# A top-k attention and its MLP on one core: the last two pairs of a batch alternate by chunk, row blocks are joined across pairs

## The chip, the cores and the metric

The kernel runs on one core of a Trainium2 chip. The metric is the device time of one execution in microseconds. Before the change it is 878.69 us as the median of three runs (876.53 to 879.49).

The engines have short names in this document: PE (TensorE, matmul), DVE (VectorE), ACT (ScalarE), POOL (GpSimd) and SP (SyncE, here only a queue that issues DMAs). "PEld" is PE's loading of weights.

## What is computed

Eight batches of eight heads, 576 rows, 64 columns a head. Each row of scores keeps its 32 largest entries; the softmax over these weighs v. The heads of a row are put side by side to 512 columns, and an MLP with 2048 hidden columns and one slope per hidden column (a leaky ReLU) follows.

```python
scores = scale * np.matmul(q, k.transpose(0, 1, 3, 2))
kth = np.partition(scores, -top_k, axis=-1)[..., -top_k:-top_k + 1]
mask = scores >= kth
scores = np.where(mask, scores, -1000000000.0)
scores = scores - np.max(scores, axis=-1, keepdims=True)
attn = np.exp(scores)
attn = attn / (np.sum(attn, axis=-1, keepdims=True) + 1e-09)
return np.matmul(attn, v).astype(np.float32)
...
h = x @ w_in
g = np.maximum(h, 0.0) + alpha * np.minimum(h, 0.0)
return (g @ w_out).astype(np.float32)
```

## The kernel before

**Tiles.** Heads are handled in pairs: 32 pairs, four to a batch. A pair has nine tiles of 128 score rows by 576 columns: tiles 0 to 7 are the four 128-row chunks of its two heads in turn (`j // 2` is the chunk, `j % 2` the head), and tile 8, which the text also calls row block 8, holds the last 64 rows of both heads. There are 288 tiles, and `ORDER[n]` says which pair and which row block tile `n` is. For batches zero to six the order is pair after pair; in the last batch the four pairs are mixed by chunk.

**One tile's way.** PE computes its scores into PSUM (`scores`, L326). ACT writes `b` = scores plus a row's estimated threshold (`act_b`, L335; `NT0` is the estimate), then takes the sign of `b` with a sum over the row, which counts how many entries are above the estimate (`act_s`, the tile `h`, L341), and later the exponential `e` (`act_e`, L346). POOL makes a sign flag `SG` of the count (`side_of`, L351). DVE makes `y` from `b` and `SG` (`flip`, L357), takes the eight largest of six segments of `y` (`seg_ops`, L367), merges them (`merge_ops`, L382 and L384), picks the row's exact limit (L395 to L411) and writes the mask `mk` (L431). POOL multiplies mask and exponential to the weights `w` (L441; DVE does it for the last six tiles, L438). SP issues a DMA that transposes two tiles of `w` (L454; L449 and L450 for row block 8). PE multiplies the transposed weights with v, and with a column of ones that gives the row's sum (`av`, tile `pu`, L489); DVE takes the reciprocal of the sums (`av_rz`, L506 and L508), and ACT scales the product into `xb` (`av_out`, L518). `x_turn` has SP issue the transposes of `xb` into `xT`, the MLP's input.

**Turns.** The order of all instructions is written out by hand: a loop over turns `n` (L765) emits, for each engine, the steps due in that turn. Turn `n` has the scores of a following tile, `b` and `h` of tile `n`, `y` of tile `n - 1`, the segments of tile `n - 2`, the merge of tile `n - 3`, and mask and weights of tile `n - 7`. Each engine works through its own list in that order and waits only where an operand or a buffer is not ready, so ACT and PE may run ahead of DVE. That distance is called ACT's lead.

**Units.** `act_b` and `act_e` run on units of one or two tiles. Before, a unit never crosses from one pair to the next, so nine tiles make four units of two and one of one (in the last batch some of row block 8 are joined). Scores of a unit are issued in the turn before it. Units of two share five buffers of `b` and four of `e`; units of one have a buffer of each of their own.

**Preparation of a pair.** `prep_plan` transposes q and k (`pe_q`, `pe_k`, `pe_t`, copied by `act_q`, `act_k`, `act_t` into one of `NQ = 5` buffers `qkT`), estimates the thresholds (`pe_g` to `dve_6`), and converts v (`act_v`). The list `ts` has the turn of each step relative to the pair's base turn `BASE[p]`. Slot "dvx" stands behind `flip` in a turn of DVE, slot "dve" ahead of it. Loads of q and k are issued 18 turns and loads of v (`load_v`) 13 turns ahead of the base turn, v into two stages in turn.

**The MLP.** Its steps wait in a queue `back`, one block of rows after another: `ph` steps (the hidden columns, L644, with ACT's `gT`, L650) and `pz` steps (the output, L658 and L662, with ACT's `o_sb`, L667). `feed(lim)` puts every block whose rows are complete into the queue. The loop takes one step a turn, and from turn 254 on up to two, within a credit of 1.9 us a turn. Batch six has two blocks of 256 rows and leaves 64 rows, which form a block with 64 rows of the last batch. `tail_of` plans the products, reciprocals, outputs and transposes of a tile after its weights, and calls `feed`. For batch six before: chunks 0 and 1 are complete with tile 3 of pair 27, the rest with its tile 8.

**PSUM.** `ps_s` has two tiles of two banks for scores; `ps_m` and `ps_a` have one bank each, for the MLP and for the preparation; `ps_d` has two banks for `pu`, `pr0`, `pr1` and `st`.

## Time and profile before

| | |
|---|---|
| runs | 876.53, 879.49, 878.69 us; median 878.69 us |
| the profiled execution | 875.27 us, its span 873.2 us |
| mean granted PE clock | 0.919 |
| matmuls, weight loads | 5747, 5747 |
| HBM read, written | 36.71 MB, 9.44 MB |

The span runs from the first to the last instruction of the profiled execution. "Busy" is time in which an engine executes; a row of a view of groups gives the source line, the engine, the operation, what is written and read, the count, then the busy time, the mean of one in ns, and behind the second bar the idle time just before these instructions and what ended it. In a view in order of time a row gives start, duration, engine, line and operation; the bracket at its end holds the idle time before it and what ended that. In a view of waits the columns are the sum, the number and the longest.

### The profile page before, as it was taken

The numbers are of one execution on the slowest core, as the hardware profiler recorded it, in microseconds if no ns is written. First come the engines' busy times: TensorE is split into PE (matmuls) and PEld (weight loads), VectorE is DVE, ScalarE is ACT, GpSimd is POOL, SyncE is SP. The second block draws the span as 40 slices with busy tenths as digits, with TensorE's granted clock in tenths as the row PEclk, the third lists the DMA queues.
The fourth block names the chain that finished last, engine by engine and source line by source line (L and its number), as shares of the span: only waits on it lengthen the run. The fifth ranks groups of instructions, "written<-read, shape, count | busy, mean of one in ns | idle before, by whom it ended". The sixth has DMA issues, their size and how long they took to land.

```text
span 873.2 us, 20627 instructions
## 1 busy us (share of the span) xinstructions
PE 725.9 (83%) x5747; PEld 426.9 (49%) x5747; DVE 833.7 (95%) x5185; ACT 789.7 (90%) x1873; POOL 430.1 (49%) x629
## 2 busy tenths in 40 slices
PE   6677687878968799878997789977897989899995
PEld 4344454434544355544454345634455555556663
DVE  4999999999999999999999999999999999999990
ACT  6999999899999999899998999999999999879851
POOL 1455455555545555545555554555554555555520
PEclk9666789699989999899987999999999999899998
DMA  7899644644666445555576456465456564355451
GB/s 163 154 180 204 122 96 92 128 95 88 147 129 116 90 109 120 114 117 95 118 159 116 83 104 132 104 129 101 101 118 123 112 101 100 80 96 101 81 99 41
DMA packets 343019, 99.50 MB, mean 114 GB/s; under 512 B 335200, under 2 KB 335216, under 8 KB 342896
## 3 DMA queue, kind: packets, MB, share of 16 engines
q1 hardware_dynamic: 340544, 95.71, 55.0%
q0 software_dynamic: 1152, 2.10, 1.9%
q8 instruction: 47, 0.77, 0.4%
q14 instruction: 76, 0.62, 0.3%
q10 hardware_dynamic: 1200, 0.30, 0.2%
HBM read 36.71 MB, written 9.44 MB: 53 GB/s over the span
## 4 chain that ended last, share of the span: by engine, by line
DVE 70%; ACT 13%; PE 12%; DMA 2%; issue 1%; POOL 1%; SPq 0%; DVEq 0%
DVE C L367 23%; DVE y L357 11%; DVE mk L431 10%; DVE C L384 9%; DVE L L382 8%; PE pz L662 3%; PE ps L326 3%; ACT b L335 3%; ACT h L341 3%; ACT e L346 2%; PE ph L644 2%; DVE P L244 2%; ACT gT L650 1%; DVE L L401 1%; DVE KK L405 1%
## 5 line engine op out<-in xcount | busy, mean ns | idle before, releaser
L441 POOL TENSOR_TENSOR w<-mk,e 128x576 bf16<-128x576 bf16 x250 | 318.9, 1276 | 336.5 <-DVE mk L431 183.9
L367 DVE MAX8 C<-y 128x8 f32<-128x96 f32 x1728 | 420.8, 244 | 0.1
L326 PE MATMUL ps<-qkT 64*128 64x288 f32 (+1 forms) x1280 | 253.8, 471 | 36.1 <-ACT b L335 35.9
L341 ACT ACTIVATE h<-b 128x576 bf16<-128x576 f32 x288 | 202.8, 704 | 1.6
L335 ACT ACTIVATE b<-ps,NT 128x576 f32<-128x576 f32 x288 | 202.0, 759 | 2.2 <-PE ps L326 2.1
L644 PE MATMUL ph<-xT,w_in_b 128*128 128x128 bf16 (+2 forms) x1088 | 158.5, 294 | 42.2 <-ACT gT L650 35.2
L326 PEld LDWEIGHTS ps<-qkT 64*128 64x128 f32 (+1 forms) x1280 | 133.6, 192 | 96.4 <-ACT b L335 60.1
L346 ACT ACTIVATE e<-b 128x1152 bf16<-128x1152 f32 (+1 forms) x158 | 174.1, 1102 | 0.0
L382 DVE MAX8 L<-C 128x8 f32<-128x48 f32 x864 | 163.5, 189 | 0.1
L357 DVE TENSOR_SCALAR y<-b,SG 128x576 int32<-128x576 int32 x288 | 147.1, 511 | 7.2 <-POOL SG L351 6.8
L431 DVE TENSOR_SCALAR mk<-b,KP 128x576 bf16<-128x576 f32 x282 | 143.8, 510 | 0.0
L644 PEld LDWEIGHTS <-w_in_b 128*128 128x128 bf16 x1088 | 85.7, 101 | 108.5 <-issue 80.0
L662 PE MATMUL pz<-w_out_b,gT 128*128 128x512 bf16 x576 | 138.6, 380 | 0.0
L650 ACT ACTIVATE gT<-ph 128x512 bf16<-128x512 f32 x144 | 88.0, 618 | 37.8 <-PE ph L644 37.6
L384 DVE MATCH_REPLACE8 C<-L,C 128x48 f32<-128x48 f32 x576 | 108.9, 189 | 0.0
L662 PEld LDWEIGHTS <-gT 128*128 128x128 bf16 x576 | 53.2, 98 | 70.6 <-issue 14.0
L489 PE MATMUL pu<-v_bf,wT 128*128 128x65 bf16 (+1 forms) x1600 | 69.6, 198 | 10.4 <-DMA wT<-w 6.8
L489 PEld LDWEIGHTS <-wT 128*128 128x128 bf16 (+1 forms) x1600 | 65.0, 103 | 21.4 <-DMA wT<-w 8.1
L351 POOL TENSOR_SCALAR SG<-S_all 128x1 int32<-128x1 f32 x288 | 64.6, 224 | 17.6 <-ACT h L341 17.5
L441 POOL TENSOR_TENSOR wm<-mk,e 128x576 bf16<-128x576 bf16 x32 | 40.8, 1275 | 49.9 <-DVE mk L431 47.1
L341 ACT ACTIVATION_READ_ACCUMULATOR h<-b 128x1 f32 x288 | 62.6, 217 | 0.0
L518 ACT ACTIVATE xb<-pu,rz 128x64 bf16<-128x64 f32 x224 | 54.3, 367 | 0.0
(100 smaller groups left out, 711.8 us busy)
## 6 DMA issues: line engine op xcount, KB each, us to landing
out_dram<-o_sb SPq DMA_DIRECT2D x35, 256.0 KB, 2.4
st_q<-in_q_dram SPq DMA_DIRECT2D x64, 128.0 KB, 2.9
st_v<-in_v_dram SPq DMA_DIRECT2D x64, 128.0 KB, 2.6
kst<-in_k_dram SPq DMA_DIRECT2D x62, 128.0 KB, 2.7
w_stage<-in_moe_w_out_dram SPq DMA_DIRECT2D x16, 256.0 KB, 3.1
w_in_b<-in_moe_w_in_dram POOLq DMA_DIRECT2D x8, 256.0 KB, 6.2
wT<-w SPq DMA_TRANSPOSE x128, 3.3
st_q<-in_q_dram SPq DMA_DIRECT2D x32, 32.0 KB, 2.7
```

Of the source, the lines that this page charges most:

```text
L326: nc.tensor.matmul(o_, l_, r_, start=True, stop=True)
L335: nc.scalar.activation(t["b"].rearrange("p (a c) -> p a c", a=2), t["ps"], AF.Identity, bias=NT0[:, p * TPP + j:p * TPP + j + 1], scale=ON ...
L341: nc.scalar.activation(h, tiles[n]["b"], AF.Sign, accum_out=S_all[:, n:n + 1])
L346: nc.scalar.activation(e, tiles[n0]["bu"], AF.Exp, scale=scl)
L357: nc.vector.tensor_scalar(t["y"].bitcast(I32), t["b"].bitcast(I32), FLIP, SG[:, n:n + 1], ALU.bitwise_xor, ALU.bitwise_xor)
L367: return [lambda g=g: nc.vector.max(out=C[:, n % TPP, g, :], in_=t["y"][:, g * SEG:(g + 1) * SEG]) for g in range(NSEG)]
L382: ops.append(lambda r=r, src=src: nc.vector.max(out=L[:, 8 * r:8 * r + 8], in_=src))
L384: ops.append(lambda r=r, src=src: nc.vector.match_replace(out=C2, in_to_replace=L[:, 8 * r:8 * r + 8], in_values=src, imm_value=NEG))
L431: nc.vector.tensor_scalar(t["mk"], t["b"], row_limit(n), None, ALU.is_ge)
L441: nc.gpsimd.tensor_tensor(dst, t["mk"], t["e"], ALU.mult)
L644: nc.tensor.matmul(hold[f][:, i, :], w_in_b[:, kk, (f + i) * 128:(f + i + 1) * 128], xT[:, kk, c0:c0 + tb], start=(kk == 0), stop=(kk == N ...
L662: nc.tensor.matmul(pz[0:m], hold["gT"][:, f, r0:r0 + m], w_out_b[:, f, :], start=False, stop=(f == NFT - 1))
```

## The change

1. `ORDER`: pairs 26 and 27 (`PA`, `PA + 1`), the last two of batch six, alternate by chunk: tiles 2i and 2i+1 of pair 26, the same of pair 27, for i from 0 to 3; then row block 8 of both.
2. `av_alt`, `rz_alt` and `out_alt` handle one chunk of both pairs at a time (20 matmuls in one `pu` bank), and `tail_of` transposes each chunk at once and feeds the MLP behind chunks 1, 3 and 4.
3. Units are two tiles throughout, except tile 8 of the first pair and the last tile; they cross pairs. `b` has five and `e` four buffers of two tiles, and none of one.
4. `NQ = 6`, one stage for v instead of two, loads of v issued later where the stage demands it, alpha's stage taken from the pool `stage`, `pr0` of the last pair in the pool `ps_a`.
5. `dve_6` in slot "dvx" of turn -3 instead of "dve" of turn -2; `act_v` of pair 1 in its turn -4 instead of 1.

```diff
-    st_vs = [prep.tile([128, 10, D], FP32, name=f"st_v{i}", bufs=1) for i in range(2)]
+    st_v = prep.tile([128, 10, D], FP32, name="st_v", bufs=1)
...
-    NQ = 5
+    NQ = 6
...
-    ORDER = [divmod(n, TPP) for n in range(N0)]
+    ORDER = [divmod(n, TPP) for n in range(N0 - 2 * TPP)]
+    PA = P0 - 2
+    ORDER += [(p, 2 * i + h) for i in range(4) for p in (PA, PA + 1) for h in range(2)]
+    ORDER += [(PA, 8), (PA + 1, 8)]
...
-        m = 1 if ORDER[n][1] == 8 and ORDER[n + 1][1] != 8 else 2
+        m = 1 if n in (8, NT - 1) else 2
...
-            if nm == "pr0":
+            if nm == "pr0" and p < NPAIR - 1:
...
-            ts = [-9, -8, -7, -6, -5, -4, -3, -2, -2, -2, -2, -2, -1, -1, 1]
+            ts = [-9, -8, -7, -6, -5, -4, -3, -2, -2, -2, -2, -2, -1, -1, -4]
...
-            ts = [-14, -13, -12, -11, -10, -9, -7, -6, -5, -5, -4, -4, -3, -2, -8]
+            ts = [-14, -13, -12, -11, -10, -9, -7, -6, -5, -5, -4, -4, -3, -3, -8]
...
-                 dict(dve=[dve_6]), dict(act=[act_v])]
+                 {dvx: [dve_6]}, dict(act=[act_v])]
...
-        b = attn.tile([128, m, S], FP32, name=f"b{m}", bufs=5 if m == 2 else 1)
+        b = attn.tile([128, 2, S], FP32, name="b", bufs=5)
...
-        e = attn.tile([128, m, S], BF16, name=f"e{m}", bufs=4 if m == 2 else 1)
-        nc.scalar.activation(e, tiles[n0]["bu"], AF.Exp, scale=scl)
+        e = attn.tile([128, 2, S], BF16, name="e", bufs=4)
+        nc.scalar.activation(e[:, 0:m, :], tiles[n0]["bu"], AF.Exp, scale=scl)
...
+    def av_alt(i):
+        m = 128 if i < 4 else 64
+        pul[i] = pu = ps_d.tile([128, 4, V1], FP32, name="pu", tag="pd")
+        for s in range(2):
+            d = pairs[PA + s]
+            for side in range(2):
+                cs = slice(0, 128) if i < 4 else slice(64 * side, 64 * side + 64)
+                av_one(pu[0:m, 2 * s + side, :], d, d["wT", i] if i < 4 else d["wTm"], side, cs)
+
+    def rz_alt(i):
+        m = 128 if i < 4 else 64
+        rz = attn.tile([128, 6], FP32, name="rz", bufs=4)
+        nc.vector.reciprocal(rz[0:m, 0:4], pul[i][0:m, :, D])
+        pul[i] = pul[i], rz
+
+    def out_alt(i):
+        m = 128 if i < 4 else 64
+        pu, rz = pul.pop(i)
+        dst = xb[B - 2][i] if i < 4 else xm[B - 2]
+        for c in range(4):
+            nc.scalar.activation(dst[:, 256 + 64 * c:320 + 64 * c], pu[0:m, c, 0:D], AF.Copy,
+                                 scale=rz[0:m, c:c + 1])
...
-            a16 = mlp.tile([NFT, 128], FP32, name="a16", bufs=1)
+            a16 = mlp.tile([128, DM], FP32, name="a16", tag="stage", bufs=3)[0:NFT, 0:128]
...
-            if wp < P0:
+            if wp in (PA, PA + 1):
+                if (wj == 8 or wj % 2) and wp == PA + 1:
+                    i = wj // 2
+                    put(n + 3, "pe", lambda: av_alt(i))
+                    put(n + 4, "dve", lambda: rz_alt(i))
+                    put(n + 6, "act", lambda: out_alt(i))
+                    put(n + 6, "end", lambda: x_turn(b, (i,)))
+                    if i in (1, 3, 4):
+                        lim = (b + 1) * S if i == 4 else b * S + 128 * i + 128
+                        put(n + 8, "end", lambda: feed(lim))
+            elif wp < P0:
...
-        load_v(1)
...
+            if n == 1:
+                load_v(1)
...
-                if n == max(0, BASE[p] - 13):
+                if n == max(BASE[p] - 13, BASE[p - 1] - 7 + 4 * (p == 2)):
```

More of the change, by code (lines that the diff above doesn't have):

```diff
@@ L119, in early_sets @@
             nc.gpsimd.memset(ksts[i][64:128, 4, :], 0.0)
-        for t_ in st_vs:
-            nc.vector.memset(t_[64:128, 4, :], 0.0)
-            nc.vector.memset(t_[0:64, 5, :], 0.0)
+        nc.vector.memset(st_v[64:128, 4, :], 0.0)
+        nc.vector.memset(st_v[0:64, 5, :], 0.0)
         for t_ in v_bfs:
@@ L200, in act_v @@
         def act_v():
-            nc.scalar.copy(d["v"][:, :, 0:D], d["st_v"])
+            nc.scalar.copy(d["v"][:, :, 0:D], st_v)
         def pe_k():
```

5 lines of the change are left out of this document (2 added, 3 removed).

## The prediction

> **What bounds the kernel now.** I read the page's busy shares first, then busy time by stretch, then what VectorE (DVE) waits for, then TensorE (PE) and ScalarE (ACT) in order of time around 760 us.
>
> ```profile
> span 873.2 us, 20627 instructions
> PE 725.9 (83%) x5747; PEld 426.9 (49%) x5747; DVE 833.7 (95%) x5185; ACT 789.7 (90%) x1873; POOL 430.1 (49%) x629
> ...
> 20.00:100.00 80.00, 58.37 (x353) 34.73 (x351) 77.53 (x477) 79.18 (x177) 40.59 (x61) 0.65 0.92 172
> ...
> 300.00:400.00 100.00, 85.53 (x669) 48.04 (x668) 100.00 (x630) 92.94 (x228) 53.07 (x76) 0.95 0.55 111
> ...
> 740.00:770.00 30.00, 25.91 (x243) 17.43 (x239) 29.80 (x189) 25.69 (x59) 15.68 (x24) 0.89 0.40 85
> 770.00:800.00 30.00, 27.18 (x210) 17.05 (x207) 28.69 (x173) 26.57 (x59) 15.90 (x25) 1.00 0.58 104
> 800.00:830.00 30.00, 29.99 (x315) 19.49 (x314) 29.42 (x182) 26.46 (x54) 15.73 (x22) 1.00 0.46 88
> ```
>
> The stretches' columns are PE, PE loads, DVE, ACT and POOL busy, then PE's granted clock. DVE has no gap in the middle of the kernel (100.00 of 100 us). What DVE does not use lies at the start, in the stretches from 740 us on, and behind its last product. So an edit can shorten the kernel only where it removes DVE work, a DVE wait, or a piece of the end. ACT with 92.94 us and PE with 85.53 us in the middle are hidden behind DVE. The waits of DVE, by the instruction that waited; the first row is from 20 to 50 us, the next two from 50 to 100 us (and what PE itself waited for there), then one row for 100 to 740 us and two for 740 to 850 us:
>
> ```profile
> DVE y L357 <- POOL SG L351: 2.4, 1, 2.4
> ...
> DVE rz L506 <- PE pu L489: 1.0, 1, 1.0
> DVE P L244 <- PE pr L236: 0.4, 1, 0.4
> ...
> PE pu L489 <- DMA wT<-w: 3.5, 1, 3.5
> ...
> L357 DVE TENSOR_SCALAR y<-b,SG 128x576 int32<-128x576 int32 x224 | 114.2, 510 | 0.1
> ...
> L357 DVE TENSOR_SCALAR y<-b,SG 128x576 int32<-128x576 int32 x35 | 17.9, 512 | 1.3 <-POOL SG L351 1.1
> ...
> L535 DVE RECIPROCAL rz<-pu 128x4 f32<-128x4 f32 (+1 forms) x9 | 1.5, 171 | 0.8 <-PE pu L489 0.8
> ```
>
> One y per tile: 640 us for 224 tiles is 2.86 us of DVE a tile, which is the length of a turn of the hand-written order. Late DVE waits sum to 1.3 + 0.8 = 2.1 us; after the start-up (y of the first tiles) only 2.4, 1.0 and 0.4 us more are lost. How far ACT is ahead of DVE comes from counting ACT's h and DVE's y begun by 738, 768 and 790 us:
>
> ```profile
> L341 ACT ACTIVATE h<-b 128x576 bf16<-128x576 f32 x254 | 179.1, 705 | 1.5
> L357 DVE TENSOR_SCALAR y<-b,SG 128x576 int32<-128x576 int32 x252 | 128.7, 511 | 5.9 <-POOL SG L351 5.7
> ...
> L341 ACT ACTIVATE h<-b 128x576 bf16<-128x576 f32 x264 | 186.0, 705 | 1.5
> L357 DVE TENSOR_SCALAR y<-b,SG 128x576 int32<-128x576 int32 x263 | 134.3, 511 | 6.1 <-POOL SG L351 5.9
> ...
> L341 ACT ACTIVATE h<-b 128x576 bf16<-128x576 f32 x271 | 190.9, 704 | 1.6
> L357 DVE TENSOR_SCALAR y<-b,SG 128x576 int32<-128x576 int32 x271 | 138.4, 511 | 7.1 <-POOL SG L351 6.8
> ```
>
> The lead is two tiles at 738 us, one at 768 and none at 790: this is the only place after the start where ACT and PE cannot keep up, and it is where the change moves the MLP of batch six (counted from zero). PE there, in order of time, with two stretches:
>
> ```profile
> 747.79 1.62 PE L326 MATMUL ps<-qkT 64*64 64x288 f32 x12
> ...
> 752.13 1.86 PE L326 MATMUL ps<-qkT 64*128 64x288 f32 x8 [1.32 <-ACT b L335]
> 756.77 2.92 PE L326 MATMUL ps<-qkT 64*128 64x288 f32 x8 [2.77 <-ACT b L335]
> 759.62 3.11 PE L644 MATMUL ph<-xT,w_in_b 128*128 128x256 bf16 x16
> ...
> 769.34 0.80 PE L489 MATMUL pu<-v_bf,wT 128*128 128x65 bf16 x20
> 770.07 1.24 PE L326 MATMUL ps<-qkT 64*128 64x288 f32 x8
> 771.24 1.92 PE L644 MATMUL ph<-xT,w_in_b 128*128 128x256 bf16 x16
> ...
> 784.02 2.98 PE L662 MATMUL pz<-w_out_b,gT 128*128 128x512 bf16 x13
> ...
> 750.00:762.00 12.00, 7.91 (x32) 4.67 (x31) 11.80 (x74) 11.12 (x26) 6.44 (x10) 0.72 0.59 119
> 762.00:774.00 12.00, 11.16 (x128) 8.66 (x127) 12.00 (x77) 9.58 (x23) 6.79 (x10) 1.00 0.44 65
> ```
>
> Between two blocks of the MLP, PE has nothing but scores, sits idle (1.32 and 2.77 us), its clock falls to 0.72, and the same eight score matmuls take 2.92 instead of 1.24 us, the same sixteen ph 3.11 instead of 1.92 us. Then two blocks come at once.
>
> **The change part by part.** Durations are from this execution, 875.27 us with its span of 873.2 us. The median of the runs shown, 878.69 us, lies 3.42 us higher; I put the sum on the execution and move the result to the median.
>
> *Batch six fed by chunks.* In the order of the instructions the two 256-row blocks start in turns 258 and 266 instead of 262 and 268, because pairs 26 and 27 finish a chunk every four turns. PE's work per four turns, by the rows above (0.12 us per ph, 0.229 per pz, 0.04 per pu matmul, scores 1.24 a unit, 1.62 with a tile of row block 8), against 4 x 2.86 = 11.4 us of DVE:
> - Before, turns 258 to 261: scores only, 2.5. Then 262 to 265: 64 ph 7.7 + 50 pu 2.0 + scores 3.4 = 13.1; 266 to 269: 40 pz 9.2 + 2.5 + 0.8 = 12.5. PE falls behind by 2.8 us in eight turns, after losing 1.7 + 1.2 + 0.6 = 3.5 us to the clock in the gap.
> - After, 258 to 261: 64 ph 7.7 + 40 pu 1.6 + scores 2.9 = 12.2; 262 to 265: 34 pz 7.8 + 1.6 + 3.2 = 12.6; 266 to 269: 6 pz and 56 ph 8.1 + 0.8 + 2.5 = 11.4; 270 to 273: 34 pz and 8 ph 8.8 + 3.3 = 12.1; 274 to 277, last batch's 128-row block: 10.4. Behind by 2.0 after eight turns, 2.7 at the worst.
>
> So the trough is the same size but is not preceded by a lost 3.5 us, and not by a rest either. Starting from a lead of one tile or a little less, DVE still touches zero. I keep half of the waits: -1.0 us. Ends: -2.1 (all gone), and +0.8: before, a tally of 2.8 us used up a lead of two tiles, at most 5.7 us and by my estimate 4.8, so ACT and PE waiting for one another cost 2 us that the tally does not see; 2.7 + 2 with a lead of 1.8 makes 2.9 us of waits instead of 2.1.
>
> What is queued behind: chunks' x transposes stand on SP four turns before the first ph that reads them (three before), among the transposes of w, and hold them only until ACT has written the chunk, on which ACT is ahead. Same number of transposes.
>
> *Chunk-wise attention products.* Five av of 20 matmuls instead of two pairs of 20 and 30: equal matmuls, equal ACT outputs (20). DVE loses one reciprocal: six (two of the row's form and a small one for each pair) become five:
>
> ```profile
> L506 DVE RECIPROCAL rz<-pu 128x4 f32<-128x4 f32 x56 | 8.0, 144 | 1.0 <-PE pu L489 1.0
> ```
>
> -0.1 us, on the path since DVE is the bound there.
>
> *Row blocks two by two across pairs.* Thirteen pairs of single exponentials become double ones:
>
> ```profile
> L346 ACT ACTIVATE e<-b 128x1152 bf16<-128x1152 f32 x130 | 155.3, 1194 | 0.0
> L346 ACT ACTIVATE e<-b 128x576 bf16<-128x576 f32 x28 | 18.9, 673 | 0.0
> ```
>
> 13 x (2 x 673 - 1194) = 2.0 us of ACT over the whole kernel, hidden by DVE: 0. The lead pays nothing, it grows; bounds 0 and -0.4 (the 0.4 us wait of P between 50 and 100 us, where ACT is busiest, 79.18 of the 80 us from 20 us on). The threshold of a pair's first tile is now needed one turn earlier and is written one turn earlier (dve_6): 0.
>
> *Fewer buffers.* b for ten tiles instead of eleven, e for eight instead of nine. An exponential now waits for POOL's product seven tiles back:
>
> ```profile
> L441 POOL TENSOR_TENSOR w<-mk,e 128x576 bf16<-128x576 bf16 x250 | 318.9, 1276 | 336.5 <-DVE mk L431 183.9
> ```
>
> That product ends, by my count of turns, 1.3 us and a mask after a turn's start, three turns before the y of the unit's second tile: ACT can lead by 3 x 2.86 less about 1.9, so 6.5 us. The lead counted above, two tiles or at most 5.7 us, is under it: 0. If the lead were clipped where a block starts, it would be clipped where it is longest, and DVE would wait only for what a dip takes beyond 6.5 us; no row after 100 us shows even a wait with today's dips.
>
> *One v stage, alpha in the stage pool, load_v later, act_v of pair 1 earlier.* SP issues v of pair 1 after q and k of pair 2; ACT reads it four turns later, so the transposes of w behind it on SP (the first in turn 8) see a queue that is free again. One v copy moves from turn 10 to turn 5 on ACT; its cover is ACT's lead over DVE there. Two memsets less, while DVE waits for the first pair anyway. 0; with the cover gone, one copy:
>
> ```profile
> L201 ACT CAST v_bf<-st_v 128x640 bf16<-128x640 f32 x32 | 23.2, 730 | 1.3 <-DVE NT L286 1.3
> ```
>
> +0.7 us; the other end is -0.4, for the 2.4 us wait at the start if SP's earlier alpha took something off it.
>
> *Six qkT buffers, pr0 of the last pair in another bank*: needed by the new order, no instruction more: 0.
>
> *The end.* The last six tiles, their products and the last block keep their order:
>
> ```profile
> 848.52 4.50 DMA wT<-w
> ...
> 857.24 5.55 PE ph L644 x64
> ```
>
> The end from the last product at 848.5 us is a chain of transposes and one block that waits for no backlog: 0.
>
> Sum: -1.0 - 0.1 = -1.1 us: 874.2 us by the profiled execution, **877.6 us** by the median. Own range, from -2.2 and +0.8: 876.5 to 879.5.
>
> **A rule against the row.** The Trainium skill, "TensorE: Matmul & The Clock Gate", section "The HAM clock gate (the "warmup" mystery)", says that PE drops to half rate after an idle window of about 3.4 us. No single wait in the rows above reaches it (1.32, 2.77 us), yet the clock read 0.72; the measurement decides, and I take the gaps as the cause. By the letter the slow stretch would have another cause and stay, and the 12.2 us of turns 258 to 261 would take 12.2 / 0.72 = 16.9 us, a way into the third rival.
>
> **The rivals.**
> 1. *All waits go* (faster). With PE never idle at 750 us and ACT 2 us lighter, late waits of 2.1 vanish and those between 50 and 100 us (1.0 + 0.4) too: -2.1 - 0.1 - 1.4 = -3.6, 875.1 us. For: the 3.5 us that PE lost to its clock, and ACT's small lead in the first 100 us. Against: the 1.0 us goes back to PE's wait for a transpose of w, not to ACT, and PE's tally stays behind DVE's.
> 2. *The early feed does nothing.* ph would wait for its xT: no chunk gains, 878.6 us. Against: in the late stretch PE waited for xT nowhere but at the last chunks, with three turns of room.
> 3. *ACT and PE set the pace from turn 258* (slower). Between 768 and 790 us ACT did seven tiles in 22 us, 3.14 us a tile. If it keeps that pace for all sixteen turns 258 to 273, DVE loses 16 x (3.14 - 2.86) = 4.5 us, and the gap that restored the lead is gone. Less a lead under 0.3 us, and with 0.8 us of waits left behind it, waits become 5.0 instead of 2.1: +2.9 - 0.1, 881.5 us. It decides when the lead at turn 258 is under a tenth of a tile. For: ACT carries six gT, four outputs and two units in turns 258 to 261. Its units show what that is:
>
> ```profile
> 774.23 1.09 ACT L650 ACTIVATE gT<-ph 128x512 bf16<-128x512 f32 x2
> 775.18 1.39 ACT L335 ACTIVATE b<-ps,NT 128x576 f32<-128x576 f32 x2
> 779.00 0.28 ACT L390 ACTIVATE ra<-S_all,c 128x3 f32<-128x3 f32 x1
> ```
>
> Two gT take 0.95 us and a unit 3.8, so 2.9 + 7.6 + about 1.6 for outputs and the small ones = 12.1 us against 11.4. Against: the pace of 3.14 came while PE ran two blocks at once.
>
> **How the numbers follow.** About 0.3% (2.6 us) is what can be told from no change. Forecast 0.42 and rival 2 0.10 lie inside: same 0.52. Rival 1 0.28: faster. Rival 3 0.20: slower. The range reaches to rivals 1 and 3, widened by the 0.4 us of the small unknowns: 874.6 to 882.0 us.
>
> **What would show it.** Right: PE's clock in the stretch 750 to 762 us near 1.0 and its busy share near 12 of 12; sixteen ph of the first block at 1.9 us; DVE waits after 740 us about 1 us; the middle at 100 of 100. The chunk step is wrong if DVE's y waits for POOL's SG in 755 to 800 us by more than 2 us. The buffer step is wrong if ACT's e shows idle time before POOL and DVE shows any between 100 and 740 us. The whole is wrong if the end behind the last product is not 24 to 25 us, or if DVE's busy sum moves by more than 1 us from 833.7.

## The result and the profile after

The change makes the kernel slower: 885.53 us as the median of nine runs (882.32 to 893.02), beside 878.03 us (876.53 to 882.11) for the kernel before on the same chip. The ratio of the runs is 1.0069, 95% interval 1.0046 to 1.0091, so about 6.1 us (4.0 to 8.0); the two medians are 7.5 us apart. The profiled execution took 885.53 us; its span is 10.6 us longer than the one shown of before, whose execution, at 875.27 us, was faster than all nine runs.

The head of the page of the kernel after:

```profile
span 883.8 us, 20598 instructions
PE 746.4 (84%) x5747; PEld 426.7 (48%) x5747; DVE 835.5 (95%) x5182; ACT 788.3 (89%) x1860; POOL 431.0 (49%) x629
```

With the same 5747 matmuls PE is busy 20.5 us longer, and with three instructions fewer DVE is busy 1.8 us longer; ACT saves 1.4 us. Busy time by stretch (columns as in the prediction) and DVE's waits from 100 to 740 and from 740 to 850 us:

```profile
300.00:400.00 100.00, 89.06 (x687) 48.72 (x687) 100.00 (x624) 91.16 (x221) 52.41 (x75) 0.93 0.56 113
400.00:500.00 100.00, 83.44 (x637) 45.62 (x637) 97.40 (x608) 93.42 (x231) 50.07 (x71) 0.93 0.58 115
740.00:770.00 30.00, 29.32 (x281) 19.22 (x278) 29.88 (x184) 26.86 (x61) 15.65 (x23) 1.00 0.50 98
750.00:762.00 12.00, 12.00 (x85) 5.97 (x82) 11.88 (x79) 9.40 (x26) 6.93 (x11) 1.00 0.55 87
770.00:800.00 30.00, 29.88 (x226) 17.36 (x224) 26.21 (x163) 26.02 (x59) 14.75 (x22) 1.00 0.46 85
...
DVE y L358 <- POOL SG L352: 3.1, 2, 2.6
...
DVE rz L559 <- PE pu L490: 3.7, 1, 3.7
```

The PE clock at 750 us is 1.00 and PE has no gap there, as forecast. But DVE now loses 2.6 us in the middle of the kernel (97.40 of 100), and one 3.7 us wait between 770 and 800 us.

To see where the 10.6 us lie, I cut each trace by the starts of DVE's y of tiles 36, 252 and 287. Before, the cuts are at 119.8, 738.0 and 838.7 us; after, at 122.8, 746.1 and 848.6 us. So 3.0 us come before tile 36, 5.1 in the middle (618.2 us becomes 623.3), 1.8 in the late stage (100.7 becomes 102.5) and 0.75 behind the last y. The first, third and fourth of these are in large part chance, or can't be told from it. Experiments 9 and 10, which do the same work there as the kernel before or a little more, reach tile 36 at 121.4 and 121.1 us. The late stage takes 102.9, 100.9 and 102.0 us in experiments 6, 9 and 10, which have it as before; behind the last y it takes 34.9 and 33.0 us in 6 and 9, beside 34.5 before and 35.2 after.

### Three readings of the trace

**The joined unit is dear.** PE in order of time in the middle of the kernel before (row block 8 alone), then in the kernel of experiment 14, where the same tiles are multiplied alone:

```profile
384.50 1.24 PE L326 MATMUL ps<-qkT 64*128 64x288 f32 x8
390.68 1.19 PE L326 MATMUL ps<-qkT 64*64 64x288 f32 x8
```

```profile
393.16 1.24 PE L328 MATMUL ps<-qkT 64*128 64x288 f32 x4
395.56 1.19 PE L328 MATMUL ps<-qkT 64*64 64x288 f32 x8
```

Eight matmuls of two ordinary tiles, one for each side of the pair and so on different halves of PE's rows, take 1.24 us; the four of a single tile, all on one half, take 1.24 us as well. So two on different halves run at once, and two on one half do not. A unit that joins row block 8 with an ordinary tile would so cost about 1.24 + 1.19 us; at full clock it takes 2.69 us in the traces. Here is one in the kernel after that met half clock, with what stood around it (pk is a transpose for a later pair):

```profile
390.61 1.02 PE L668 MATMUL ph<-xT,w_in_b 128*128 128x512 bf16 x4 [1.23 <-ACT gT L674]
392.33 1.02 PE L207 MATMUL pk<-ident_f,kst 128*128 128x128 f32 x4 [0.70 <-ACT qkT L199]
393.29 4.89 PE L327 MATMUL ps<-qkT 64*128 64x288 f32 x12
398.11 1.61 PE L668 MATMUL ph<-xT,w_in_b 128*128 128x512 bf16 x4
399.76 0.60 ACT L674 ACTIVATE gT<-ph 128x512 bf16<-128x512 f32 x1 [3.93 <-PE ph L668]
403.61 0.52 DVE L358 TENSOR_SCALAR y<-b,SG 128x576 int32<-128x576 int32 x1 [2.60 <-POOL SG L352]
```

```profile
388.00:391.00 3.00, 1.77 (x28) 1.40 (x27) 3.00 (x21) 3.00 (x9) 1.63 (x3) 1.00 0.84 147
391.00:393.00 2.00, 1.30 (x7) 0.72 (x5) 2.00 (x16) 2.00 (x6) 1.31 (x2) 0.87 0.32 73
393.00:395.00 2.00, 2.00 (x6) 0.79 (x6) 2.00 (x15) 2.00 (x5) 1.15 (x1) 0.50 0.77 148
395.00:398.00 3.00, 3.00 (x10) 0.79 (x6) 3.00 (x21) 0.83 (x2) 1.81 (x4) 0.50 0.26 58
```

PE had little to do for five microseconds (1.77 + 1.30 us), its clock had fallen to 0.50 by the time the unit ran, and the twelve matmuls took 4.89 us. The ph behind them came late, ACT stood still for 3.93 us, and DVE, whose supply had shrunk, waited 2.60 us. From the unit on PE to the late y on DVE it is ten microseconds.

**dve_6 was free where it stood.** DVE and POOL in the same turn of the kernel before, and of experiment 6, which moves dve_6 (the row `NT<-sq`) and nothing else:

```profile
392.31 0.51 DVE L431 TENSOR_SCALAR mk<-b,KP 128x576 bf16<-128x576 f32 x1
392.96 1.28 POOL L441 TENSOR_TENSOR w<-mk,e 128x576 bf16<-128x576 bf16 x1 [1.12 <-issue]
394.20 0.23 POOL L351 TENSOR_SCALAR SG<-S_all 128x1 int32<-128x1 f32 x1
394.39 0.14 DVE L286 TENSOR_SCALAR NT<-sq 128x9 int32<-128x9 int32 x1
394.46 0.52 DVE L357 TENSOR_SCALAR y<-b,SG 128x576 int32<-128x576 int32 x1
```

```profile
395.51 0.16 DVE L286 TENSOR_SCALAR NT<-sq 128x9 int32<-128x9 int32 x1
395.59 0.50 DVE L431 TENSOR_SCALAR mk<-b,KP 128x576 bf16<-128x576 f32 x1
396.23 1.27 POOL L441 TENSOR_TENSOR w<-mk,e 128x576 bf16<-128x576 bf16 x1 [1.20 <-issue]
397.48 0.22 POOL L351 TENSOR_SCALAR SG<-S_all 128x1 int32<-128x1 f32 x1
397.73 0.52 DVE L357 TENSOR_SCALAR y<-b,SG 128x576 int32<-128x576 int32 x1
```

In this turn y waits for a round trip: mk on DVE, w on POOL, SG behind it on POOL, y. From mk to y it takes 2.15 us before (394.46 - 392.31) and 2.14 after. Before, dve_6 ran inside that time; moved ahead of mk it delays the whole trip by 0.08 us, once in each pair. It doesn't look like a wait, because y starts 0.03 us behind SG's end and DVE counts as busy: the only trace of it is the busy sum.

**The late stage and the tail.** The kernel after around 780 us (PE, then one row of DVE), then PE around 850 us:

```profile
777.99 2.69 PE L327 MATMUL ps<-qkT 64*64 64x288 f32 x12
780.62 1.04 PE L682 MATMUL pz<-w_id_b,xT 128*128 128x512 bf16 x4
781.49 0.81 PE L686 MATMUL pz<-w_out_b,gT 128*128 128x512 bf16 x3
782.14 0.80 PE L490 MATMUL pu<-v_bf,wT 128*128 128x65 bf16 x20
782.98 0.18 DVE L559 RECIPROCAL rz<-pu 128x4 f32<-128x4 f32 x1 [3.67 <-PE pu L490]
```

```profile
846.11 0.49 PE L490 MATMUL pu<-v_bf,wT 128*128 128x65 bf16 x10 [0.33 <-DMA wT<-w]
852.23 3.57 PE L668 MATMUL ph<-xT,w_in_b 128*128 128x128 bf16 x32 [5.63 <-DMA xT<-xb]
855.60 1.27 PE L490 MATMUL pu<-v_bf,wT 128*128 128x65 bf16 x20
```

The reciprocal at 783 us waits for attention products that stand behind a joined unit at full clock and seven pz. At 846 us PE has no MLP left to work on, waits 5.63 us for a transpose, and does the next 32 ph in 3.57 us instead of some 1.95; the attention products behind them are late in turn.

### The profile page after: what moved, and what is told of

The parts are those of the page before. It is cut to its first block, busy times and chain, and to the rows that moved or that the text cites. A ratio compares the mean times of both kernels' runs of the same rounds, so it can differ in the third digit from the quotient of the medians.

```text
span 883.8 us, 20598 instructions
## 1 busy us (share of the span) xinstructions
PE 746.4 (84%) x5747; PEld 426.7 (48%) x5747; DVE 835.5 (95%) x5182; ACT 788.3 (89%) x1860; POOL 431.0 (49%) x629
## 5 line engine op out<-in xcount | busy, mean ns | idle before, releaser
L327 PE MATMUL ps<-qkT 64*128 64x288 f32 (+1 forms) x1280 | 271.4, 482 | 9.6 <-ACT b L336 9.3
L342 ACT ACTIVATE h<-b 128x576 bf16<-128x576 f32 x288 | 208.4, 724 | 0.9
L674 ACT ACTIVATE gT<-ph 128x512 bf16<-128x512 f32 x144 | 90.6, 638 | 40.7 <-PE ph L668 40.5
L342 ACT ACTIVATION_READ_ACCUMULATOR h<-b 128x1 f32 x288 | 68.3, 237 | 0.0
L519 ACT ACTIVATE xb<-pu,rz 128x64 bf16<-128x64 f32 x208 | 50.5, 368 | 0.0
```

The lines of the kernel that those rows point to most:

```text
L327: nc.tensor.matmul(o_, l_, r_, start=True, stop=True)
L342: nc.scalar.activation(h, tiles[n]["b"], AF.Sign, accum_out=S_all[:, n:n + 1])
```

## The experiments

Eighteen kernels ran, each beside the kernel before on the same chip. The table puts the main readings together: the ratio to before with its interval, busy sums of PE and DVE, and, worked out from all of DVE's rows in the one trace of each kernel, DVE's idle time (gaps over 0.08 us) between the y of tile 36 and of tile 252 and the length of that stretch. "Busy PE" stands for idle products, matmuls whose results nobody reads.

```
                                 ratio  (95% interval)     PE     DVE   waits  36-252
before                           1                        725.9  833.7   0.00  618.2
after                            1.0069 (1.0046, 1.0091)  746.4  835.5   3.07  623.3
 1 units kept in a pair          1.0033 (1.0012, 1.0054)  720.8  835.2   0.34  620.4
 2 before + joined units, dve_6  1.0043 (1.0021, 1.0065)  746.4  836.1   4.11  624.4
 3 no alternation                1.0037 (1.0018, 1.0056)  746.4  835.7   4.34  624.5
 4 other order of matmuls        1.0118 (1.0072, 1.0163)  748.3  836.1   8.81  629.5
 5 dve_6 back                    1.0075 (1.0051, 1.0098)  749.7  833.8   6.58  625.4
 6 before + dve_6 moved          1.0016 (0.9999, 1.0033)  729.5  836.3   1.58  621.9
 7 row blocks 8 paired           1.0047 (1.0027, 1.0067)  712.3  835.6   2.15  621.8
 8 as 11, late products first    1.0035 (1.0018, 1.0052)  724.8  833.4   0.00  618.3
 9 before + dearer row block 8   1.0003 (0.9982, 1.0024)  739.4  833.8   0.88  619.3
10 before + busy PE at the end   1.0002 (0.9980, 1.0024)  731.6  833.7   0.00  618.2
11 alternation alone             1.0053 (1.0029, 1.0077)  723.0  833.7   0.12  618.5
12 as 11, busy PE at the end     0.9996 (0.9975, 1.0017)  724.5  833.3   0.15  618.5
13 as 3, five buffers of e       1.0016 (0.9994, 1.0037)  745.2  835.4   0.24  620.3
14 as 3, joined units split      1.0030 (1.0010, 1.0050)  749.9  835.7   2.37  622.6
15 after, split, dve_6, busy PE  1.0028 (1.0008, 1.0047)  758.4  833.9   5.45  624.2
16 as 17, joined units split     1.0012 (0.9992, 1.0031)  744.3  834.3   4.61  623.6
17 as 13, dve_6 back             1.0029 (1.0007, 1.0050)  744.8  833.9   4.39  623.0
18 after, five buffers of e      1.0058 (1.0031, 1.0085)  737.8  835.3   0.48  620.7
```

Two things can be read from the last columns. They come from one execution of each kernel, which is not always a typical one (13's took 878.05 us beside a median of 880.99, 15's 887.38 beside 882.26), so it is the groups that count. Taking the waits off the stretch leaves 618.2 to 618.4 us in every kernel with dve_6 at its old place and no joined units, 618.6 to 619.0 in those with joined units, and 620.1 to 620.7 wherever dve_6 is moved (7 has a reason of its own): about 2 us for 24 pairs. And the eight kernels without joined units (before, 1, 6, 8 to 12) wait 0.4 us on average, none over 1.6, while the eleven with mixed units (after, 2 to 5, 13 to 18) wait 0.24 to 8.81 us, 4.0 on average. A mixed unit is one that joins row block 8 with an ordinary tile.

**1 to 3: which part.** Theory 1 put the loss on the joined units, theory 2 on the alternation with its early feed. Experiment 1 takes the joined units out of the kernel after, and gives the lone exponential its own buffer back:

```diff
-        m = 1 if n in (8, NT - 1) else 2
+        m = 1 if ORDER[n][1] == 8 and ORDER[n + 1][1] != 8 else 2
...
```

> All of the change except that a unit no longer crosses from one pair to the next (row block 8 alone again, the last pairs' row blocks 8 together). Theory 1, joined score units: a unit of row block 8 and another tile takes 2.69 us of PE at full clock, where before the row block alone took 1.19 and the other tile half of 1.24, so 0.9 us more in some 22 units and the lead of ACT shrinks. Then PE's busy sum falls from 746 to about 726 us, the DVE waits at 401 and 508 us go, and the time is 877 to 880 us (about 6 us under the changed kernel). Theory 2, the alternation and the early feed: the time stays above 882 us, with the 3.7 us wait of a reciprocal near 779 us and the 1.35 us near 855 us still there. Theory 3, fewer buffers: b has still ten tiles here, e again nine, so a time between the two.

Experiment 2 puts the joined units, their buffers and the moved dve_6 into the kernel before.

> The kernel before with units that cross pairs (and their buffers and the step dve_6 as changed), nothing else. Theory 1: PE's busy sum rises by about 18 us, ACT's lead falls, and the time is 4 to 7 us over the kernel before. Theory 2: the time stays within 1.5 us of the kernel before, since the last pairs are as they were.

Experiment 3 takes the alternation, `av_alt` and its helpers and the early feed out of the kernel after (the first lines of the change's diff on `ORDER` undone).

> The changed kernel with pairs 26 and 27 one after the other and batch six fed as before; crossing units, six buffers and the rest stay. Theory 1: 882 to 885 us, the DVE wait near 401 us still there. Theory 2: 878 to 880 us, since the waits near 779 and 855 us (5 us) go.

The three came out at 882.15, 883.45 and 882.91 us beside 879.18: each holds half of the loss or somewhat more. Without joined units DVE's waits in the middle are gone but for 0.34 us; with them they are there, alternation or not. So neither theory is enough alone, and experiment 1, which by theory 1 should be back at before's time, stays 3.0 us above it.

**4: the order of the matmuls.** The twelve matmuls of a joined unit were put in an order in which the two halves of PE's rows take turns as long as both have work (the keys of the sort replaced by the half, and a loop that alternates).

> The changed kernel with the score matmuls of a unit ordered so that the two halves of PE's rows take turns as far as they can. In a joined unit four of six matmuls use the same half. If the count sets the time (theory 1 by count), four slots of 0.62 us remain: 2.5 instead of 2.69 us a unit, PE busy falls by at most 5 us, and the time stays within 2 us of the changed kernel. If the order sets it (theory 1 by order), three slots of 0.62, 1.9 us, PE busy falls by some 18 us and the time falls to about 879 us.

The ratio, 1.0118, is the largest of all. Where the clock is full, a joined unit that begins with row block 8 takes 2.35 us (427.99 us in its trace), less than 2.69; but one that begins with an ordinary tile takes 3.17 us, at a clock of 1.00:

```profile
242.79 3.17 PE L333 MATMUL ps<-qkT 64*128 64x288 f32 x12
242.80:245.97 3.17, 3.17 (x14) 1.30 (x14) 3.17 (x23) 3.14 (x7) 1.63 (x4) 1.00 0.62 138
```

By the starts of its single matmuls, the ordinary tile's products run alone there, although small products of the other half stand right behind them. So the new order gains nothing even at full clock (PE is busy 748.3 us, beside 746.4), and with the clock down the burst at 188.6 us lasts 5.84 us, and DVE waits 4.67 us behind it.

**5 and 6: dve_6.** Theory 3, as it is meant from here on, came from the rows above: dve_6 costs 2 us where it now stands. Experiment 5 puts it back in the kernel after (shown), experiment 6 moves it in the kernel before:

```diff
-            ts = [-14, -13, -12, -11, -10, -9, -7, -6, -5, -5, -4, -4, -3, -3, -8]
+            ts = [-14, -13, -12, -11, -10, -9, -7, -6, -5, -5, -4, -4, -3, -2, -8]
...
-                 {dvx: [dve_6]}, dict(act=[act_v])]
+                 dict(dve=[dve_6]), dict(act=[act_v])]
```

> The kernel after with dve_6 alone back at its old place (slot dve of turn -2, between the last MAX8 of a tile and y); all else as after. Theory 3 (moving dve_6 costs 0.073 us in each pair, because y waits for the chain mk, POOL w, POOL SG, whose length hid dve_6 before): DVE busy falls from 835.5 to about 833.5 us, and the time by about 2.2 us against after's 885.5, so about 883. Theory 1 and 2 (joined units and the early feed are all there is; dve_6 is free at either place): time as after, 885 to 886, DVE busy 835.5. DVE waits at 401 and 779 us stay under every theory.

> The kernel before with dve_6 alone moved (slot dvx of turn -3). Theory 3: about 2.2 us slower than before (ratio 1.0025), DVE busy about 836 instead of 833.7, and no DVE wait over 0.3 us that before does not have. Rival: dve_6 is worth nothing, ratio 1.000.

DVE's busy sum moved as expected in both (833.8 and 836.3 us). The time did so only in experiment 6, and there its interval (-0.1 to +2.9 us) takes in nothing as well as the 2.2 us expected. In the kernel after, the 2 us that DVE saves come back as waits (6.58 us in the middle instead of 3.07): where PE and ACT set the pace, a faster DVE only waits longer. How much of the difference is that, and how much the chance described under 13 to 18, one trace of each can't tell. Nor do the other runs show a gain: with dve_6 back the ratio is 1.0053 beside 1.0033 (11 and 1, neither with waits in the middle to speak of) and 1.0029 beside 1.0016 (17 and 13). None of these steps is clear of its interval. So the 2 us are in DVE's rows; that they are in the time isn't shown.

**7: row blocks 8 with each other.** In every second pair row block 8 comes first, so that joined units hold two row blocks 8 or two ordinary tiles; no alternation, dve_6 back.

```diff
+        ORDER += [(p, j) for j in ((8, *range(8)) if p and p % 2 == 0 else range(9))]
...
```

> The kernel after without the alternation and the early feed, dve_6 back, and every second pair taking its row block 8 first, so that a joined unit holds two row blocks 8 (16 small matmuls, 2.16 us) or two ordinary tiles (8 matmuls, 1.24 us), never a mixture (12 matmuls, 2.69 us). The units, buffers and ACT's work are those of after. Theory 1 (the mixed unit is what makes crossing dear): PE busy falls from 746 to about 726 us, the waits of DVE at 193, 401 and 508 us are gone, and the time is about before's, 877 to 880. Rival (crossing costs by its buffers or by the order of ACT, whatever the shapes): PE busy falls all the same, but the time stays 3 us above before, 881 to 883, with DVE waits in the middle.

PE fell to 712.3 us and no wait in the middle is over 0.4 us, yet the time is 884.16 us. One reason lies on POOL, in the turn shown above:

```profile
397.78 0.30 POOL L447 TENSOR_TENSOR wm<-mk,e 128x64 bf16<-128x64 bf16 x1
398.05 0.22 POOL L351 TENSOR_SCALAR SG<-S_all 128x1 int32<-128x1 f32 x1
398.31 0.52 DVE L357 TENSOR_SCALAR y<-b,SG 128x576 int32<-128x576 int32 x1
```

Row block 8 has a second, small product on POOL. It used to fall into a long turn; now it stands between w and SG in a turn that is just the round trip, and y comes 0.2 us later. By the median distance of y to y the eighteen turns of two pairs take 51.56 us instead of 51.30, 3.1 us over twelve double pairs. Its late stage is long as well (104.2 us, 5.3 of them DVE's idle time). So the experiment shows that the long waits go with the mixture, but not what the time would then be.

**8, 11 and 12: the alternation alone, and its tail.** Experiment 11 is the kernel after with units kept in a pair and dve_6 back. Experiment 8 has, besides, the attention products ahead of the MLP's steps behind the last tile (`run(n, "pe")` moved up for `n >= NT`). Experiment 12 adds to 11 idle products, whose results nobody reads, where PE waits for xT:

```diff
+            if f == 0:
+                for _ in range({256: 14, 384: 10}.get(t0 - t7 - 64, 0)):
+                    nc.tensor.matmul(ph, w_in_b[:, 0, 0:128], w_in_b[:, 0, 0:512],
+                                     start=True, stop=True)
```

> The kernel after with units kept inside a pair, dve_6 back, and in the turns behind the last tile the attention products ahead of the MLP's steps on PE. Theory 2 (at the end PE runs out of its backlog, waits 5.5 us for xT, works at half clock, and the last products stand behind ph): DVE's wait of 1.30 us at 850 us in the first such kernel goes, with theory 3 DVE busy falls by 2.2 us, so 882.15 - 1.3 - 2.2 = about 878.6. Rival: the tail's length is set by the transposes of xb, not by the order on PE, so only the 2.2 us of dve_6 come back: about 880.

> The kernel after with units kept inside a pair and dve_6 back: of the change, the alternation with its early feed and the stages of v and alpha are left. If dve_6 (2.2 us) is real wherever DVE is the bound, 882.2 - 2.2 = about 880, DVE busy 833.5, and the rest over before is the end (about +1.5 us from the last y on, PE 5.5 us without work). Rival (the early feed costs in the late stage whatever dve_6 does): about 882.

> The kernel before this one in the list, with idle products ahead of the two blocks at the end that wait for xT (14 ahead of the one behind 5.5 us of waiting, 10 ahead of the last). If the alternation loses at the end only through the half clock behind that wait, both losses go: 1.3 to 2 us at the first and 1.5 to 2 at the second, so about 876.5, and under the kernel before with a warm end. Rival (the wait for xT itself is what costs): it gains only the 1.5 to 2 us of the last block, about 878.5.

Experiment 11 was not at 880 but at 883.16 us; 8 at 882.45; 12 at 878.59. The middle of all three is the kernel before's (618.3 to 618.5 us). PE in 12 at the place where it waited 5.63 us in the kernel after:

```profile
839.41 3.18 PE L668 MATMUL ph<-w_in_b 128*128 128x512 bf16 x14
845.19 1.95 PE L672 MATMUL ph<-xT,w_in_b 128*128 128x128 bf16 x32 [2.60 <-DMA xT<-xb]
```

With the 14 idle products ahead, the 32 ph take 1.95 us, the full rate, although a wait of 2.60 us remained. From the last y to the last instruction of an engine it takes 30.2 us in 11, 29.2 in 12, and 33.0 in 8: in these traces the idle products win 1.0 us there, and putting the attention products first loses. The rest of what the two traces of 11 and 12 differ by is not in the part that differs: they part at the beginning (tile 36 at 123.1 and 120.9 us), where both do the same. By the runs, though, 12 is 4.6 us faster with intervals that do not meet, and one trace of each doesn't show where more than the 1.0 us would come from.

**9 and 10: controls on the kernel before.** Experiment 9 does one score product of a lone row block 8 twice; experiment 10 puts ten idle products ahead of the last block.

```diff
+                        if unit_of[n0][1] == 1 and hf + side == 0:
+                            mm.append(mm[-1])
```

> The kernel before with one score product of each lone row block 8 done twice (the same values into the same place), so that a pair costs PE 0.6 to 0.9 us more, as a mixed unit does in the kernel after; nothing else differs. Theory 1 (what crossing costs is PE's time in the mixed unit, which stands ahead of other products and takes ACT's lead): PE busy goes from 726 to 742 to 750 us, DVE gets waits of 1 us and more in the middle (100 to 740 us) that before does not have, and the time rises by 2 to 4 us. Rival (PE has 14% of slack in the middle and hides it): time as before, the middle at 100 of 100.

> The kernel before with ten idle products (128x512, bf16, into the bank that the first real product overwrites) ahead of the last block's first ph, where PE waits 2.69 us for xT. If the half clock behind that wait is what makes the last 64 ph take 5.55 us instead of 64 x 0.055 = 3.5, the time falls by 1.5 to 2.0 us, to about 878. If the end is set by something else, no change. Up to the last product it is the kernel before, so it shows as well how far the first 40 tiles vary from execution to execution: 0 to 2 us later than in the first profile.

Experiment 9 went against theory 1 as it was put: PE busy rose by 13.5 us to 739.4, and the time did not move (0.9982 to 1.0024). PE's sum alone did not do it. The dearer unit takes 1.67 us at full clock, and no burst of scores in the middle lasts over 3.14 us. That points to the length of a burst and its place. Experiment 10 gains nothing: the ten idle products took 3.83 us at the half clock (857.85 us) and reached past the transpose they were to cover, so that the 64 ph took 3.75 us instead of 5.55 but began later.

**13 to 18: buffers or the burst.** What was left was why the waits come and go. Experiments 13, 17 and 18 give the joint exponential a fifth buffer (`name="e", bufs=5`, with `NQ = 5` to make room), 14 to 16 split the scores and `act_b` of a mixed unit over two turns:

```diff
+            elif n in mixed:
+                scores(n, (n + 1,))
...
+                    if n0 in mixed:
+                        act_b1(n0, (1,))
```

> The third experiment's kernel (after without the alternation and the early feed) with five buffers of e instead of four and five of transposed q and k instead of six. Buffer theory (ACT's lead is held down by the joint exponential's buffers): ACT's waits for POOL go, the lead of ACT rises to 4 to 6 us between the dips as in before, DVE's waits at 193 and 301 us go, and the time falls by 3 us against that kernel's 882.9. Burst theory (both products of a mixed unit in one turn): time and waits as in that kernel, 882 to 884.

> The kernel after with five buffers of e instead of four, and five of transposed q and k instead of six to make room. Buffer theory: DVE's waits at 401 and 507 us (3.1 us) go, and the time falls by about 3 us against after's ratio of 1.0069, to 1.003 to 1.004 of before; ACT's waits for POOL go. Rival (the mixed unit's 2.69 us on PE): waits in the middle and the ratio stay, 1.006 to 1.008.

> The eighth experiment's sibling: the kernel after without the alternation, with five buffers of e and of transposed q and k, and dve_6 back. If buffers and dve_6 are what the joined units lose by, nothing is left in the middle: DVE busy 833.5 to 834, no wait over 1 us between 130 and 740 us, time as before, 879 to 881 (ratio 0.999 to 1.001). Rival (with dve_6 back DVE only waits more, since PE and ACT set the pace): as the kernel with dve_6 moved, 881, with 1 to 3 us of DVE waits in the middle.

(The sibling meant is experiment 13.)

> The same kernel as the third experiment's, but the two tiles of a mixed unit have their scores and their b in two turns, one each; the joint exponential and the buffers stay. Burst theory: DVE's waits at 193 and 301 us go, ACT's lead rises to 3 us and more, and the time falls to before's plus the 2.2 us of dve_6, about 880 to 882; the form of 12 products in 2.69 us is gone from PE. Buffer theory: waits stay, 882 to 884.

> As the one before, and the scores of the mixed units split over two turns. Buffer theory: ACT's waits for POOL (8.0 + 0.9 us with four buffers) go, ACT's lead rises over 5 us, DVE's waits at 488 and 510 us go, and the time is that of before, 879 to 881. Rival: those waits come from PE (reciprocals that wait for pu), and stay: 881 to 882.

(The one before is experiment 17.)

> The kernel after with mixed units split over two turns, dve_6 back, and idle products on PE ahead of the last two blocks that wait for xT. If the three causes are all that the change loses by, its time is that of before within 0.3%, 877 to 881; if the burst was not the cause, about 882 to 884.

The traces of 13 and 18 have no waits in the middle, as the buffer theory wanted, but 17 has the same buffers and waits 4.39 us, and the time of 18 stays at 1.0058. The larger part of what the traces with and without waits differ in is a single unit. PE and DVE in experiment 3, PE and DVE in 17, then PE in 18 and 13 at the place of experiment 3; and last, from the kernel after, the same unit one batch before the one at 393.29 us:

```profile
186.77 4.89 PE L324 MATMUL ps<-qkT 64*128 64x288 f32 x12
197.10 0.52 DVE L355 TENSOR_SCALAR y<-b,SG 128x576 int32<-128x576 int32 x1 [3.86 <-POOL SG L349]
```

```profile
498.44 4.89 PE L324 MATMUL ps<-qkT 64*128 64x288 f32 x12
509.03 0.52 DVE L355 TENSOR_SCALAR y<-b,SG 128x576 int32<-128x576 int32 x1 [2.47 <-POOL SG L349]
```

```profile
183.75 2.69 PE L327 MATMUL ps<-qkT 64*128 64x288 f32 x12
```

```profile
184.40 2.69 PE L324 MATMUL ps<-qkT 64*128 64x288 f32 x12
```

```profile
290.06 2.69 PE L327 MATMUL ps<-qkT 64*128 64x288 f32 x12
```

The unit comes once in a batch, about every 104 us. Where PE's clock is down when it runs, it takes 4.89 us and DVE waits 2.5 to 4.1 us some ten microseconds later. That holds for all five of the long waits behind a unit of 12 in its plain order (after, 2, 3, 5, 17). Where the clock is up, it takes 2.69 us and less follows, but not always nothing: no wait over 0.3 us in 13, up to 0.5 us in the kernel after, in 3 and in 18, and 0.8 to 1.4 us in 2, 17 and 5.

Whether the clock is down looks like chance. In the kernel after the unit comes at 185.9, 290.1, 393.3, 500.7 and 603.3 us, each time behind 3.05 to 3.08 us of PE work in the last five and no pause over 1.25 us; four times it takes 2.69 us and once 4.89. So the waits move from place to place. Another mixed unit of the batch (159.9, 263.7, 367.7 us in the kernel after) takes 3.3 to 4.9 us in these traces and does no harm: the lead is 2 us or more there. The split units of 14 to 16 have no such burst (none over 3.06 us), and their largest wait in the middle is 2.1 us; but they wait more often, about half of it for pu, and PE is as busy as with the units whole, since a lone tile cannot use the other half of PE. Nor is a gain in time shown: 1.0030 beside 1.0037 (14 and 3), 1.0012 beside 1.0029 (16 and 17), within the intervals. Experiment 15, all three remedies on the kernel after, reached 1.0028, not before's time. No kernel was clearly faster than before; 12, at 0.9996, is equal to it.

## Why the prediction was wrong

- **What bounds the kernel.** DVE, as read. What the reading missed is that the distance between DVE and the other two is a stock that the middle of the kernel needs: the start of y behind the end of h of its tile falls to 0.4 to 0.8 us once in each batch in the kernel after, where it stayed at 1.7 us or more in the trace of before (tiles 45 to 233, worked out from h's end and y's start of each tile).
- **Row blocks two by two across pairs: this is the step that failed.** The prediction took the 2.0 us of ACT and wrote "The lead pays nothing, it grows". It priced the ACT side alone and did not ask what the new pairs of tiles do on PE's halves. A mixed unit is 2.69 us, 4.89 at half clock, in place of shares of 1.24 and 1.19; PE's work grew by 20.5 us, the lead shrank, and DVE waits some 4 us on average in the middle, beside 0.4 without mixed units. The bounds of this step, 0 and -0.4 us, had the wrong sign.
- **The same wrong price in the tally of turns 258 to 273.** "1.62 with a tile of row block 8" was read from a row at 747.79 us whose twelve matmuls are part of a unit of two row blocks 8, sixteen in all, in the last batch. With 2.69 each, PE falls behind by 1.1 us more in every stretch that holds one, and the wait of 3.7 us at 783 us stands behind such a unit; with the alternation but without mixed units (1, 8, 11, 12) no wait in the late stage is over 1.2 us. The -1.0 us did not come: DVE idles 4.3 us between the y of tiles 252 and 287, beside 2.1 before and 2.4, 3.1 and 4.0 in experiments 9, 10 and 6, which have this stage as before. With units kept in a pair, the alternation gave 2.6 to 3.7 us: no gain even then. The prediction's sign for this step, y waiting for SG by more than 2 us, did not appear (0.3 us); the wait sat at a reciprocal.
- **The clock at 750 us.** Right: busy 12.00 of 12 us, at 1.00. The gain did not reach DVE, since ACT and PE had nothing left to gain it with.
- **dve_6 one turn earlier: 0.** Wrong by some 2 us in DVE's busy time (835.5 us, beyond the 1 us that the prediction gave as a sign of being wrong). The instruction was counted, but not what it had stood behind: the round trip through POOL. What it costs in time isn't shown (experiments 5 and 6).
- **Fewer buffers: 0.** Wrong by the prediction's own sign: ACT's e waited for POOL, for 4.2 us between 100 and 740 us, and DVE waited in the same stretch. The lead was counted at 738 us alone; in the middle of the kernel before (tiles 45 to 233, from h's end to y's start) it reaches 8.1 us, over the 6.5 us that the step allowed. A fifth buffer ended ACT's wait, but 17 has it and DVE still waits 4.39 us, so the buffers are not what makes the long waits. In time the fifth buffer moved 1.0069 to 1.0058 (18) and 1.0037 to 1.0016 (13 beside 3), each within the intervals: a cost of up to 2 us is neither shown nor excluded.
- **v, alpha, qkT, pr0: 0, and chunk-wise products: -0.1.** In the middle, experiments 11 and 12 carry these and are within 0.3 us of the kernel before. In the first 36 tiles nothing can be said: the kernels' traces reach tile 36 between 119.5 and 123.8 us, whether these parts are in them or not.
- **The end: 0.** Behind DVE's last product right (24.1 us to the end of the span after, 24.7 before). Ahead of it the backlog was missing that the prediction said nobody waits for: PE lost 1.6 us to the half clock at 852 us (3.57 instead of 1.95 us). From the last y to the span's end it is 35.2 instead of 34.5 us. One trace can't settle that, but over all of them the alternation shows: 33.0 to 36.4 us (34.5 on average) in the ten kernels without it, 35.2 to 37.5 (36.1) in the six that have it and change nothing else behind the last y (after, 1, 4, 5, 11, 18).
- **The rivals.** The third had the sign and named ACT and PE as the bound; but it put them behind turn 258, while about half of the loss lies in the middle.
- **The sum.** In the two traces the middle holds 5.1 us, dve_6 with 2.0 and the waits with 3.1; the rest lies in stretches that differ by as much where the work is the same. By the runs, taking the joined units out of the kernel after brings 1.0069 to 1.0033 (experiment 1), and taking the alternation out brings it to 1.0037 (experiment 3): some 3 us each, with intervals of 2 us to each side. For the joined units the traces show how; for the alternation they show that it gained nothing in the late stage and lost 1.6 us on average behind the last y. Why the alternation alone measured 1.0053 in one set of runs and 1.0035 and 0.9996, with changes at its end, in the others stays open, and so does what dve_6 adds to the time.

**Halves and clock.** The Trainium skill, "TensorE: Matmul & The Clock Gate", section "The mechanism", says that small matmuls run together if they use different groups of PE's rows; the rows of 4 and 8 matmuls, both 1.24 us, agree, while the units of 3.17 us in experiment 4 do not: there a product of one half stands next to a small one of the other, and they run one behind the other. The Trainium skill, the same page, section "What's actually happening", has the clock judged over a free-running window, so that one kernel differs from run to run; that the same unit takes 2.69 us four times and 4.89 once in one trace, behind nearly the same work, agrees with that.

## What to carry to other kernels

Price a regrouping on every engine that sees it: here joining two exponentials on ACT made a unit of 2.69 us on PE out of two of 1.24 and 1.19, and the long waits stood behind that unit when it met half clock, whatever PE's sum. A busy share of 100% on one engine says nothing of how small the lead of the others gets; look for where it is least, and ask what a single late burst does there. Before an instruction is moved, look at what it hides behind: a round trip to another engine shows neither as a wait nor as work.

## What the runs showed of the hardware

- PE's clock fell to half without one long pause: before the unit at 393.29 us PE was busy 3.07 of 5.00 us, its longest pause 1.23 us. Four times out of five the clock stayed up behind nearly the same work.
- Products with 64 rows on one half of PE do not overlap: 4 on one half take 1.24 us, 8 on both halves 1.24 us, and 12 with both kinds 2.69 us (2.35 or 3.17 us in experiment 4, by which kind comes first).
- The start of the kernel varies by itself: DVE idles 4.0 to 8.1 us between 20 us and tile 36, and two kernels that are the same up to some 839 us (11 and 12) reach tile 36 2.2 us apart. One trace of each kernel overstates or hides differences of that size; before's was the second earliest of twenty.
